# A reordered opening in a fused attention and MLP kernel: loads, memsets, one small copy and some transposes change their place

## The chip, the core and the metric

The kernel runs on one core of a Trainium2 chip. The core has TensorE (matmuls, PE in the profile), VectorE (DVE), ScalarE (ACT), GpSimd (POOL) and SyncE (SP), which only issues DMAs. Each engine works through its own instructions in the program's order; semaphores tie the engines together. The metric is the device time of the program in microseconds (us), over several executions.

## The reference

q, k and v are (8 batches, 8 heads, 576 positions, 64), f is (8, 8, 576); w_in is (512, 2048), w_out is (2048, 512), all float32.

```python
scores = q @ k.T / sqrt(64)                  # for each batch and head
cum = cumsum(log(clip(f, 0.0001, 1.0)))      # along the positions
scores = where(later position, -1e9, scores + cum[i] - cum[j])
attn = exp(scores - max); attn /= sum(attn) + 1e-9
x = (attn @ v), heads side by side           # (4608, 512)
h = x @ w_in
out = (h - tanh(h)) @ w_out                  # (4608, 512)
```

## The kernel before

**Pairs of heads.** The unit of attention is a pair of heads; a batch has four pairs (`NPAIR`), and `pairs` lists 32 of them in order. A pair's scores are computed transposed, positions of k on the partitions, in seven tiles (`TILES`): tiles 0 to 2 belong to the pair's first head, tile 3 holds the last 64 columns of both heads, tiles 4 to 6 belong to the second. `scores` (L337) makes one tile: matmuls of K^T and Q^T (L352), for batch 0 a matmul that adds the causal mask `late` (L355), and an exponential on ScalarE into a tile `e`, or `el` for tile 3 (L361). From batch 1 on GpSimd masks the tile instead (L371). `values` (L382) multiplies the tiles of the pair before with v (L389); VectorE divides by the sums (L398 to L400) into `xn`. `turn` (L407) transposes `xn` into `XR`, the input of the MLP: in batch 0 with TensorE (L417) and a copy on VectorE (L419) or ScalarE (L421), later by DMA.

**The decay in the matmul.** K^T and Q^T have 67 rows: 64 of the head and three more, which add the decay. For every head but the first of batch 0 the rows are filled by DMA from `chi` and `clo`, which are computed for all 64 heads at once: clip of f (L181), logarithm on ScalarE (L184), cumulative sum (L187), `chi` (L189), `clo` (L190). For head 0 three rows of `clo` are copied straight into `KT[0]` (L191), and ScalarE writes the rows of `QT[0]` (L572).

**How Q^T and K^T come about.** In the early part (pairs 0 to 4 and some more) `trans` (L287) transposes q or k of a pair with six TensorE transposes (L298) into one PSUM bank, and two copies (four, if split) bring it to `QT` or `KT`: the letters of its argument `copies` give each copy's engine, V for VectorE (L311), A for ScalarE (L309). With "VA" or "Vv" only the first copy is issued at once, and the others wait in `LATER` until `rest()` issues them.

**The order of work** is written out by hand. After some set-up, `start()` (L570) runs pair 0's transposes and its tiles 0 and 1, with filler matmuls (`unread`, whose results nobody reads). `bulk()` (L209) issues the remaining loads of batch 0. Then, for each pair p, `att_items(p)` (L591) lists what is emitted around each of its seven tiles `ti`: the scores, loads from the table `LOADS`, transposes of later pairs, values of the pair before, turns. For p up to 3 nothing else is there; from p = 4 steps of the MLP (`mlp1`, L441; `mlp2`, L506) are spread between them, and after the last pair the MLP's rest runs alone.

**Loads.** All loads of q, k, v and the weights are DMAs of GpSimd's queue: `load_qk` (L101), `load_v_rest` (L122), `load_v_head` (L126), `load_v_block` (L130), `load_win` (L221). GpSimd is busy for 0.6 to 1.2 us with the issue of each, and its other instructions wait behind it. The order for batch 0 is: q and k of heads 0-1 and 2-3, the last 64 positions of v, v's heads 0 and 1, the mask `late` (L169), the `chi` row of Q^T (L212), q and k of heads 4-5 and 6-7, four blocks of v. `last()` (L585), in pair 1, holds four memsets of GpSimd that batch 1 and `EL[2]` need.

Of the kernel before, what the change touches and what calls it, by code (L numbers as in the profile page):

```python
# [14 lines left out]
PITCH = 640  # L15
VW = 66
# [5 lines left out]
def kernel(  # L22
# [10 lines left out]
    nc = tc.nc  # L33
    P = 128
# [87 lines left out]
    def load_v_rest(b):  # L122
        nc.gpsimd.dma_start(out=vn[b % 2][0:S % P, NJ - 1, :, 0:D],
                            in_=v[b, :, S - S % P:S, :].rearrange("h p d -> p h d"))
# [40 lines left out]
    EL = [cst.tile([P, 192], FP16, tag=f"el{i}", name=f"el{i}") for i in range(3)]  # L165
    load_v_rest(0)
    load_v_head(0, 0)
    load_v_head(0, 1)
# [10 lines left out]
    for e in EL[0:2]:  # L179
        nc.vector.memset(e, 0.0)  # L180
    nc.vector.tensor_scalar(out=lf, in0=lf, scalar1=0.0001, scalar2=1.0,  # L181
                            op0=ALU.max, op1=ALU.min)
    nc.vector.memset(vn[0][:, :, :, D:VW], 1.0)
# [7 lines left out]
    nc.vector.tensor_copy(out=KT[0][NH:NX, 0, 0:S], in_=clo[NH:NX, :])  # L191
# [17 lines left out]
    def bulk():  # L209
        (k_hi, chi_0), (k_lo, clo_0), (q_hi, _) = aug_rows(0)  # L210
        nc.sync.dma_start(out=k_hi, in_=chi_0)
        nc.gpsimd.dma_start(out=q_hi, in_=chi_0)  # L212
        nc.sync.dma_start(out=k_lo, in_=clo_0)
        load_qk(qn, q, 0, 4, 6)
        load_qk(kn, k, 0, 4, 6)
        load_qk(qn, q, 0, 6, H)
        load_qk(kn, k, 0, 6, H)
        for n in range(NJ - 1):
            load_v_block(0, n, 2, H)
# [5 lines left out]
    def load_wout(e0, e1):  # L225
# [4 lines left out]
             (1, 0): [lambda: load_win(0, DFF // 2)],  # L230
# [56 lines left out]
    def trans(b, c, src, dst, early, copies, split=False):  # L287
# [26 lines left out]
        now = 1 if copies in ("VA", "Vv") else 2  # L314
# [255 lines left out]
    def start():  # L570
        unread(47)
        nc.scalar.activation(out=QT[0][NH:NX, 0, :], in_=cum[NH:NX, :], func=AF.Identity, bias=add_q[NH:NX, :], scale=mul_q[NH:NX, :])  # L572
        q_rest = trans(*pairs[0], qn, QT, True, "AAAA", True)
        for fn in q_rest:
            fn()
        unread(6)
        k_rest = trans(*pairs[0], kn, KT, True, "VVVV", True)
        unread(34)
        scores(*pairs[0], 0)
        for fn in k_rest:  # L580
            fn()
        scores(*pairs[0], 1)
        unread(2)

    def last():  # L585
        nc.gpsimd.memset(KT[1][:, :, S:PITCH], 0.0)
        nc.gpsimd.memset(vn[1][D:P, NJ - 1, :, :], 0.0)
        nc.gpsimd.memset(vn[1][:, :, :, D:VW], 1.0)
        nc.gpsimd.memset(EL[2], 0.0)

    def att_items(p):  # L591
        def put(fn, *args):
            items.append((lambda: fn(*args), True))
# [6 lines left out]
        for ti in range(len(TILES)):  # L600
# [12 lines left out]
            if ti == 5 and p < NPAIR - 1:  # L613
                put(trans, *pairs[p + 2], qn, QT, True, "VV")
# [11 lines left out]
            if ti == at_k and p < 2 * NPAIR - 1 and p != NPAIR:  # L626
                put(trans, *after, kn, KT, early, "AV" if p in (0, 2) else "VV")
            if p == NPAIR:
                if ti == 0:
                    put(turn, *pairs[1])  # L630
                elif ti == 1:
                    put(turn, *pairs[p - 2])
                    put(values, *before)
                    put(mlp1, 0, 0, 0)
                elif ti == 2:
                    put(mlp1, 0, 1, 0)
                    put(turn, *before, True)
                    put(trans, *after, kn, KT, early, "Vv")
            elif early and ti in (2, 4) and before:
                put(values, *before, (ti // 2 - 1,))  # L640
            elif not early and ti == 2 and before:
                put(values, *before, (0, 1), p == NPAIR + 2)
# [71 lines left out]
```

## Time and profile before

| | |
|---|---|
| time, 3 runs | 338.72 us median (338.71 to 339.28) |
| the profiled execution | 338.77 us, of which the span (first to last instruction) is 337.1 us |
| busy in the span | PE 330.0 (98%), DVE 260.8 (77%), ACT 233.2 (69%), POOL 163.2 (48%) |
| granted TensorE clock | 1.00 |
| first scores of pair 0 on TensorE | at 9.11 us |
| first scores of pair 4 on TensorE | at 24.78 us |
| first matmul with w_in | at 27.28 us |

Times inside the profile count from the start of the span. In a timeline a row has the start, the duration from first start to last end of a run of like instructions, the engine, the line of the kernel, the operation, what it writes and reads, its shape, the number of instructions, and in brackets the engine's idle time just before it and what ended that. In the view of waits a row names who waited for whom: microseconds in total, times, longest.

### The profile page before, as it was taken

What the parts mean: (1) busy time and instruction counts of PE and PEld (TensorE: products, weight loads), DVE (VectorE), ACT (ScalarE), POOL (GpSimd) and SP (SyncE); (2) the same over time, 40 slices, a digit from 0 to 9 for tenths busy, and PEclk for the clock granted to TensorE, in tenths of its full rate; (3) what the DMA queues carried; (4) which work ended last, traced back from release to release, by engine and by line L of the source; (5) the groups of instructions that cost most, each with busy time, mean ns of one, the idle gap of its engine ahead of it and who ended that gap; (6) DMA issues with size and microseconds to landing.
All of it is one profiled execution on the core that took longest, in us unless ns stands there. A gap on an engine that the chain in (4) does not pass through costs nothing.

```text
span 337.1 us, 8726 instructions
## 1 busy us (share of the span) xinstructions
PE 330.0 (98%) x3313; PEld 235.6 (70%) x3313; DVE 260.8 (77%) x509; ACT 233.2 (69%) x438; POOL 163.2 (48%) x321
## 2 busy tenths in 40 slices
PE   8899999999999999999999999999999999999996
PEld 8775558875687558845888888656865686486485
DVE  7998986659887886778867896788668866966865
ACT  6997777978977886788677867787558733632630
POOL 8977467775667564767377637722322210000000
PEclk9999999999999999999999999999999999999999
DMA  9999999999979997999899999990130022002003
GB/s 113 143 203 202 186 198 165 184 159 172 142 87 190 136 134 72 164 152 139 94 122 187 118 112 117 163 132 18 51 113 2 19 65 97 2 31 95 0 12 116
DMA packets 147468, 38.82 MB, mean 115 GB/s; under 512 B 128181, under 2 KB 146335, under 8 KB 147426
## 3 DMA queue, kind: packets, MB, share of 16 engines
q0 software_dynamic: 94528, 18.37, 75.5%
q1 hardware_dynamic: 52892, 19.89, 32.4%
q8 instruction: 26, 0.43, 0.6%
q14 instruction: 16, 0.13, 0.2%
q10 hardware_dynamic: 6, 0.01, 0.0%
HBM read 36.85 MB, written 9.44 MB: 137 GB/s over the span
## 4 chain that ended last, share of the span: by engine, by line
PE 90%; DVE 7%; ACT 2%; issue 1%; ACTq 0%
PE hps L451 36%; PE ops L517 29%; PE ps L352 11%; PE av L389 8%; PE ops L492 4%; DVE KT L311 2%; DVE QT L311 1%; PE t L298 1%; ACT e L361 1%; DVE xn L400 1%; DVE gq L462 0%; DVE TQ L187 0%; ACT th L456 0%; PE x L417 0%; DVE clo L190 0%
## 5 line engine op out<-in xcount | busy, mean ns | idle before, releaser
L451 PE MATMUL hps<-XR,win 128*128 128x512 f16 (+1 forms) x640 | 140.7, 357 | 0.3 <-DVE gq L462 0.3
L456 ACT ACTIVATE th<-hps 128x512 f32<-128x512 f32 x144 | 86.6, 602 | 55.5 <-PE hps L451 53.5
L361 ACT ACTIVATE e<-ps 128x512 f16<-128x512 f32 x192 | 110.2, 597 | 8.9 <-PE ps L352 7.4
L462 DVE TENSOR_TENSOR gq<-hps,th 128x512 f16<-128x512 f32 x144 | 98.0, 687 | 23.6 <-ACT th L456 22.0
L371 POOL TENSOR_SCALAR_AFFINE_SELECT e<-e 128x128 f16<-128x128 f16 x168 | 60.7, 364 | 71.5 <-ACT e L361 68.7
L451 PEld LDWEIGHTS <-win 128*128 128x128 f16 x640 | 57.7, 97 | 49.0 <-issue 1.1
L352 PE MATMUL ps<-QT,KT 67*128 67x64 f16 (+4 forms) x384 | 76.5, 276 | 2.0 <-DVE KT L311 1.4
L517 PEld LDWEIGHTS <-gq 128*128 128x128 f16 x640 | 60.3, 97 | 11.1
L517 PE MATMUL ops<-wout,gq 128*128 128x256 f16 x512 | 63.2, 272 | 0.0
L352 PEld LDWEIGHTS <-KT 67*128 67x128 f16 x384 | 36.4, 98 | 23.4 <-DVE KT L311 2.0
L389 PEld LDWEIGHTS <-e 128*128 128x128 f16 x896 | 32.3, 97 | 3.6
L389 PE MATMUL av<-vn,e 128*128 128x65 f16 x896 | 33.6, 193 | 0.0
L517 PE MATMUL ops<-W,sq 128*128 128x256 f16 x256 | 31.2, 272 | 0.0
L131 POOL DMA_DIRECT2D vn<-in_v_dram x32 | 28.0, 877 | 6.5 <-DMA win<-in_moe_w_in_dram 2.9
L400 DVE TENSOR_TENSOR xn<-av,rs 128x640 f16<-128x640 f32 x32 | 26.4, 825 | 1.3 <-DVE rs L399 0.2
L517 PEld LDWEIGHTS <-sq 128*128 128x128 f16 x256 | 24.1, 97 | 3.4
L108 POOL DMA_DIRECT2D kn<-in_k_dram x25 | 21.2, 848 | 2.1 <-issue 1.8
L108 POOL DMA_DIRECT2D qn<-in_q_dram x25 | 21.2, 848 | 1.8 <-issue 1.4
L371 POOL TENSOR_SCALAR_AFFINE_SELECT el<-el 128x128 f16<-128x128 f16 x28 | 9.3, 333 | 26.1 <-ACT el L361 25.8
L398 DVE TENSOR_SCALAR rs<-av 128x10 f32<-128x10 f32 x32 | 5.2, 163 | 18.2 <-PE av L389 17.0
L532 ACT ACTIVATE m<-ops 128x512 f32<-128x512 f32 x16 | 9.5, 596 | 10.9 <-PE ops L517 10.9
L484 DVE TENSOR_TENSOR gq<-gq 128x512 f16<-128x512 f16 x32 | 17.1, 533 | 0.0
(83 smaller groups left out, 311.8 us busy)
## 6 DMA issues: line engine op xcount, KB each, us to landing
out_dram<-ost SPq DMA_DIRECT2D x34, 256.0 KB
vn<-in_v_dram POOLq DMA_DIRECT2D x24, 128.0 KB, 6.2
qn<-in_q_dram POOLq DMA_DIRECT2D x20, 128.0 KB, 5.0
kn<-in_k_dram POOLq DMA_DIRECT2D x20, 128.0 KB, 5.6
win<-in_moe_w_in_dram POOLq DMA_DIRECT2D x2, 1024.0 KB, 11.8
wout<-in_moe_w_out_dram POOLq DMA_DIRECT2D x2, 1024.0 KB, 15.6
XR<-xn SPq DMA_TRANSPOSE x56
qn<-in_q_dram POOLq DMA_DIRECT2D x6, 144.0 KB, 4.6
```

The costliest lines, as they stand in the source:

```text
L108: nc.gpsimd.dma_start(out=dst[b % 2][0:pn, n, :].rearrange("p (h d) -> p h d", h=H), in_=src[b, :, n * P:n * P + pn, :].rearrange("h p d - ...
L131: nc.gpsimd.dma_start(out=vn[b % 2][:, n, h0:h1, 0:D], in_=v[b, h0:h1, n * P:(n + 1) * P, :].rearrange("h p d -> p h d"))
L352: nc.tensor.matmul(out=ps[:, col:col + n], lhsT=kt[0:rows, h, j * P:(j + 1) * P], rhs=qt[0:rows, h, i0:i0 + n], start=True, stop=cut == 0)
L361: nc.scalar.activation(out=e[:, lo:hi], in_=ps[:, lo:hi], func=AF.Exp, bias=-SHIFT, scale=qscale)
L371: nc.gpsimd.affine_select(out=view, in_=view, compare_op=ALU.is_ge, fill=0.0, base=0, pattern=pat, channel_multiplier=-1)
L389: nc.tensor.matmul(out=av[:, a, ib, :], lhsT=E.pop((b, c, a, j, ib)), rhs=vn[b % 2][:, j, 2 * c + a, 0:D + 1], start=(j == 0), stop=(j == ib))
L400: nc.vector.tensor_tensor(out=xn.rearrange("p i (a d) -> p a i d", a=2), in0=av[:, :, :, 0:D], in1=rs.to_broadcast([P, 2, NJ, D]), op=ALU. ...
L451: nc.tensor.matmul(out=hps[:, o:o + n], lhsT=win[:, ci, ft * P:(ft + 1) * P], rhs=XR[:, ci, t:t + n], start=(ci == 0), stop=(ci == NCH - 1))
L456: nc.scalar.activation(out=th, in_=hps, func=AF.Tanh, scale=-1.0)
L462: nc.vector.tensor_tensor(out=GQ[(u, i)][:, half, kt, :], in0=hps, in1=th, op=ALU.add)
L484: nc.vector.tensor_tensor(out=LHS[name](u, i)[:, ks], in0=LHS[x](u, i)[:, ks], in1=LHS[y](u, i)[:, ks], op=op)
L517: nc.tensor.matmul(out=ps[:, m, :], lhsT=LHS[lhs](u, kt // 4)[:, kt % 4, m * P:(m + 1) * P], rhs=rhs[:, kt, :], start=(fresh and (apart or ...
```

## The change

- In the set-up, q's heads 4 and 5 are loaded first, then v's head 0, then the last positions of v. v's head 1 moves into `bulk()`, behind k's heads 4 and 5.
- All three `EL` memsets stand behind the clip of f; `last()` no longer has the third.
- The DMA of the `chi` row moves from `bulk()` to just behind `clo`, and GpSimd, not VectorE, copies the three rows of `clo` into `KT[0]`.
- The memsets of `KT[1]` and `vn[1]` move from GpSimd to VectorE; that of `KT[1]` to `start()`, between pair 0's tiles 0 and 1.
- w_in's first half is loaded in two pieces of a quarter.
- The filler ahead of the first scores has 29 matmuls in place of 34.
- Transposes: pair 2's q moves from pair 0's tile 5 to its tile 3, with its second copy issued later; pair 1's second K^T copy is issued between those two. Pair 3's and pair 4's q move from tile 5 to tile 6 of the pairs 1 and 2.
- In pair 2, the values of pair 1's first head follow tile 3, not tile 2.

```diff
-    load_v_rest(0)
+    load_qk(qn, q, 0, 4, 6)
     load_v_head(0, 0)
-    load_v_head(0, 1)
+    load_v_rest(0)
...
-    for e in EL[0:2]:
-        nc.vector.memset(e, 0.0)
     nc.vector.tensor_scalar(out=lf, in0=lf, scalar1=0.0001, scalar2=1.0,
                             op0=ALU.max, op1=ALU.min)
+    for e in EL:
+        nc.vector.memset(e, 0.0)
...
-    nc.vector.tensor_copy(out=KT[0][NH:NX, 0, 0:S], in_=clo[NH:NX, :])
+    nc.gpsimd.dma_start(out=QT[0][D + 2:D + 3, 1:H, :], in_=chi[1:H, :])
+    nc.gpsimd.tensor_copy(out=KT[0][NH:NX, 0, 0:S], in_=clo[NH:NX, :])
...
     def bulk():
-        (k_hi, chi_0), (k_lo, clo_0), (q_hi, _) = aug_rows(0)
+        (k_hi, chi_0), (k_lo, clo_0), _ = aug_rows(0)
         nc.sync.dma_start(out=k_hi, in_=chi_0)
-        nc.gpsimd.dma_start(out=q_hi, in_=chi_0)
         nc.sync.dma_start(out=k_lo, in_=clo_0)
-        load_qk(qn, q, 0, 4, 6)
         load_qk(kn, k, 0, 4, 6)
+        load_v_head(0, 1)
...
-             (1, 0): [lambda: load_win(0, DFF // 2)],
+             (1, 0): [lambda: load_win(0, DFF // 4), lambda: load_win(DFF // 4, DFF // 2)],
...
-        now = 1 if copies in ("VA", "Vv") else 2
+        now = 1 if copies in ("VA", "Vv", "Av") else 2
...
-        unread(34)
+        unread(29)
         scores(*pairs[0], 0)
         for fn in k_rest:
             fn()
+        nc.vector.memset(KT[1][:, :, S:PITCH], 0.0)
         scores(*pairs[0], 1)
...
     def last():
-        nc.gpsimd.memset(KT[1][:, :, S:PITCH], 0.0)
-        nc.gpsimd.memset(vn[1][D:P, NJ - 1, :, :], 0.0)
-        nc.gpsimd.memset(vn[1][:, :, :, D:VW], 1.0)
-        nc.gpsimd.memset(EL[2], 0.0)
+        nc.vector.memset(vn[1][D:P, NJ - 1, :, :], 0.0)
+        nc.vector.memset(vn[1][:, :, :, D:VW], 1.0)
...
-            if ti == 5 and p < NPAIR - 1:
+            if ti == 6 and 0 < p < NPAIR - 1:
                 put(trans, *pairs[p + 2], qn, QT, True, "VV")
...
-                put(trans, *after, kn, KT, early, "AV" if p in (0, 2) else "VV")
+                put(trans, *after, kn, KT, early, "Av" if p == 0 else "AV" if p == 2 else "VV")
+            if p == 0 and ti == 3:
+                put(trans, *pairs[2], qn, QT, True, "Vv")
+                items.append((rest, False))
...
-            elif early and ti in (2, 4) and before:
-                put(values, *before, (ti // 2 - 1,))
+            elif early and ti in (3 if p == 2 else 2, 4) and before:
+                put(values, *before, (ti // 4,))
```

More of the change, by code (lines that the diff above doesn't have):

```diff
@@ L165 @@
     EL = [cst.tile([P, 192], FP16, tag=f"el{i}", name=f"el{i}") for i in range(3)]
+    load_qk(qn, q, 0, 4, 6)
+    load_v_head(0, 0)
     load_v_rest(0)
-    load_v_head(0, 0)
-    load_v_head(0, 1)
     nc.gpsimd.affine_select(out=late, in_=late, compare_op=ALU.is_ge, fill=-60000.0,
```

## The prediction

> **What bounds the kernel now.** I read the page's slices first, then TensorE's waits by stretch, then the timelines of VectorE (DVE), ScalarE (ACT) and GpSimd (POOL) over the first 35 us. The slices (one digit is 8.4 us, busy tenths):
>
> ```profile
> PE   8899999999999999999999999999999999999996
> DVE  7998986659887886778867896788668866966865
> ```
>
> TensorE is full except in the first two slices and the last. From 60 us on its row in the table of windows reads 10.00 of 10.00 us up to the tail, so what the change can win or lose lies before about 50 us, and whatever it wins there stays won, since all later work follows TensorE. TensorE's waits in the windows 0:10, 10:20 and 20:30:
>
> ```profile
> PE idle L566 <- DVE warm L142: 1.1, 1, 1.1
> PE ps L352 <- DVE KT L311: 0.9, 1, 0.9
> ...
> PE ps L352 <- ACT e L361: 0.3, 1, 0.3
> PE idle L566 <- ACT el L361: 0.2, 1, 0.2
> ...
> PE ps L352 <- DVE KT L311: 0.4, 1, 0.4
> PE x L417 <- DVE xn L400: 0.2, 1, 0.2
> ```
>
> The reader should see that 0.9 (the first scores) and 0.4 both end on a copy of K^T by VectorE. In VectorE's timeline (start, duration, instruction, idle before it):
>
> ```profile
> 3.60 0.25 DVE L180 MEMSET el<- 128x96 uint32 x2
> 3.77 0.39 DVE L181 TENSOR_SCALAR TQ<-TQ 67x576 f32<-67x576 f32 x1
> 4.91 1.35 DVE L187 TENSOR_TENSOR_SCAN TQ<-TK,TQ 67x576 f32<-67x576 f16 x1 [0.66 <-ACT TQ L184]
> ...
> 7.76 0.30 DVE L191 COPY KT<-clo 3x576 f16<-3x576 f16 x1
> 8.09 1.97 DVE L311 COPY KT<-t 64x288 f16<-64x288 f16 x4
> 10.26 1.62 DVE L311 COPY QT<-t 64x576 f16<-64x576 f16 x2 [0.20 <-PE t L298]
> 12.22 0.81 DVE L311 COPY KT<-t 64x576 f16<-64x576 f16 x1 [0.34 <-ACT KT L309]
> ...
> 23.10 1.62 DVE L311 COPY KT<-t 64x576 f16<-64x576 f16 x2
> ```
>
> Between 8.09 and 24.72 VectorE idles only twice, 0.20 and 0.34 us. The last row is pair 4's K^T, and TensorE's first scores of pair 4 start at 24.78, 0.43 us late, on it. **So VectorE's queue is the bound from the first K^T copy to 24.78**; TensorE's smaller waits before that are slack. A gain at the start counts only as far as this queue ends earlier.
>
> **The change, part by part.** All times are of the profiled execution: 338.77 us, of which the span is 337.1 and 1.7 lie around it; it is 0.05 above the median of 338.72.
>
> *Start of the chain.* The two memsets of `EL` stand ahead of the clip of the decays (3.60 and 3.77 in the rows above; the clip's input was there, its wait had ended by 3.5). Moved behind, the clip starts at 3.60: 0.17 earlier. The three memsets then lie in the 0.66 idle ahead of the scan (3 x 0.14 = 0.42, with the ones of `vn` 0.12: 0.54), so the added third one costs nothing; without that cover it would cost 0.14. The scan, chi and clo follow 0.17 earlier: clo ends at 7.56 instead of 7.73.
>
> *Decay rows to GpSimd.* The copy of L191 leaves VectorE: 7.76 to 8.09 is 0.33. The K^T copies then start at 8.09 - 0.17 - 0.33 = 7.59. The scores need the first two (0.97 in all, 8.56) and the copied rows. No GpSimd copy is in this trace. Its nearest rows:
>
> ```profile
> 6.48 0.55 POOL L169 TENSOR_SCALAR_AFFINE_SELECT late<-late 128x128 f16<-128x128 f16 x1
> 7.17 0.54 POOL L212 DMA_DIRECT2D QT<-chi x1
> ...
> 17.49 0.60 POOL L586 MEMSET KT<- 67x512 f16 x1
> 18.15 0.53 POOL L587 MEMSET vn<- 64x528 f16 x1
> 18.74 0.18 POOL L588 MEMSET vn<- 128x80 f16 x1
> ```
>
> Memsets of 80 and 512 elements give 0.98 ns an element and 0.10 fixed, so 0.66 for 576. The selects of L371 (128 elements 0.30, 256 elements 0.42) give 0.73. From above, the select of `late` took 0.55 for 128 elements, beside chi on VectorE: at that rate 576 cost 2.46. I take 0.73: a select also reads and writes SBUF. Before it in GpSimd's queue stand three loads (0.68 + 0.79 + 0.71, for 0.71 + 0.77 + 0.77 now), the select and the chi row's DMA, which is done at about 7.5. The copy runs from 7.60 to 8.33, covered by the K^T copies until 8.56. First scores: 8.56 + 0.05 = 8.61 for 9.11. Five filler matmuls fewer (0.06 each) end at 7.9, inside that wait, and cost nothing.
>
> *Memsets of batch 1 to VectorE.* `KT[1]`'s stands behind pair 0's K^T copies: 0.37 from start to next start (the row of L159). Pair 1's Q^T copies could start at 8.61 + 1.14 = 9.75 (now 9.11 to 10.25); VectorE is free at 7.59 + 1.96 + 0.37 = 9.92. So the idle of 0.20 goes, and these copies start 0.33 earlier. The two of `vn[1]` (rows of L163 and L183) cost 0.31 + 0.12 = 0.43, in pair 1, with nothing to hide them. The four memsets leave GpSimd's queue (1.56).
>
> *Late turns.* Pair 2's Q^T is transposed in pair 0's tile 3, and its first copy goes ahead of pair 1's second K^T copy, which waited 0.34 for ScalarE's. That idle goes: 11.55 Q^T of pair 2, 12.37 K^T of pair 1, 13.2 the other half. Late next: pair 1's first scores, which need the K^T copy ended at 13.2. Now it ends at 13.03 and they start at 13.50, held by other waits; they can't follow the 0.5 of the start. That is a new wait of some 0.3 on TensorE, within the slack. Pair 2's K transposes behind it end near 13.25 + 0.70 = 13.95, VectorE wants them at 14.02. The turns moved from tile 5 to 6 and pair 1's values moved to tile 3 change TensorE's order inside the slack (17.2 to 24.4): nothing.
>
> *Loads.* q's heads 4 and 5, issued at 4.3 with landings there taking 4.4 to 4.8, are in by 9.1, wanted at 11. Behind the GpSimd copy are kn 4-5, v head 1, q and k 6-7, four v blocks. v head 1 moves from 5.73 to 9.0; its 4.6 to landing makes 13.6, wanted at 15.2. The last v block is issued 0.8 later (13.5), and lands between 17.6 (the DMA engines, not the issue, set it: their latency grew from 3.4 to 5.2 us here) and 18.45; wanted at about 18.5. A miss falls into TensorE's 0.30 and 0.43. w_in's half takes one issue more (0.83), paid by the memsets that left; it landed at 26.1, its first matmul is at 27.28, and the first quarter alone can land earlier. Nothing.
>
> *Sum at 24.72:* -0.33 (pair 1's copies) - 0.34 (idle) + 0.43 (memsets) = **-0.24**. TensorE's scores of pair 4 then start at 24.54, and later work keeps the distance: 338.77 - 0.24 = **338.5**. The 0.50 at the start is half spent again on VectorE's memsets.
>
> **The rivals.**
>
> *The gain is eaten (338.8).* Tile 3 of pair 0 needs the chi row of Q^T over GpSimd's queue, issued at 7.17 and 3.7 us to landing: 10.87, against a first use at 11.13. The change wants it at 10.6, and puts 144 KB in place of 64 KB ahead of it; at the windows' 166 GB/s that is up to 0.5 later. Then tile 3 stays near 11.1, pair 2's Q transposes behind it end at 11.8 instead of 11.55, and VectorE loses the 0.25. For it: the margin is 0.26 now and about none after. Against: the issue itself comes 0.2 earlier.
>
> *More than the queue allows (337.8).* If VectorE's memsets overlap its copies and TensorE's waits after 24.78 (0.16 on xn, 0.32 on gq at 33.38) go too: 0.50 + 0.48. Against: both end on VectorE's queue, and its rows show no overlap beyond 0.04.
>
> *Slower: the GpSimd copy itself (339.9).* TensorE's first scores wait for it, everything behind. Pair 1's copies start at its end + 0.05 + 1.14 once that is past 9.92, and 10.16 is where the sum is zero: a copy of over 1.4 us loses. At the rate of the `late` select, 2.46, it ends at 10.06, pair 1's copies start at 11.25, and the sum is 1.00 - 0.34 + 0.43 = +1.1. For it: that select ran beside chi and took 0.55 where the one of `id` took 0.29. Against: GpSimd's memsets at 17.5 to 19.0 ran beside VectorE's copies out of PSUM, as this copy would, and both kept their usual durations. A first use of an instruction could also cost extra; the nearest row is ScalarE's table load, 1.28, which would make the copy 2.0 and the time 339.4. The Trainium skill, GPSIMD Engine Reference, Instruction dispatch, says that the first call of a freshly loaded kernel pays some 6 us that no profile row shows; by that, as an estimate, the copy ends at 14.3 and the time is 344. The trace does not bear it out: GpSimd's first select, 0.29 us, started at 1.22, right after its input.
>
> **Chances.** Forecast 0.55 (its own range 338.4 to 338.65); eaten 0.24; more 0.09; slower by the copy 0.12, a third of that within the bound. About 0.2%, 0.68 us, is what a measurement of this kernel can tell from no change. So faster 0.09, same 0.83, slower 0.08. The range of 338.0 to 339.0 takes in the first two and half a copy's excess, and leaves out the long copy and most of the large gain.
>
> **What would show it.** L181 at 3.6; the K^T copies at 7.6; a GpSimd COPY of about 0.7 that ends before 8.6; the first scores at 8.6; no idle of VectorE until 24.5; a new wait of TensorE for K^T near 13.2; pair 4's scores at 24.5. Wrong if the copy takes over 1.4, if tile 3's scores stay at 11.1, or if TensorE waits for a v block near 18.

## The result and the profile after

| | before | after |
|---|---|---|
| time, median of 6 (lowest to highest) | 338.76 us (338.71 to 339.28) | 340.12 us (339.75 to 340.28) |
| profiled execution, its span | 338.77, 337.1 | 340.10, 338.3 |
| first scores of pair 0, first matmul | 9.12 | 9.08 |
| first scores of pair 4, first matmul | 24.78 | 25.02 |
| TensorE's idle time at L517, near 105 us | none | 0.97 |

The ratio is 1.0035 [1.0022, 1.0048] (in brackets the 95% interval): the changed kernel is slower by 1.36 us. The forecast was 338.5, and the range ended at 339.0. Between the two profiled executions the span grew by 1.2 us. Two places hold it: 25.02 - 24.78 = 0.24 in the opening, and 0.97 at 105 us, in a part of the kernel that the change does not touch and where the prediction expected nothing to move. (The 9.11 in the table of the kernel before is the start of the weight load of that first matmul.)

The busy slices of the page, TensorE and VectorE, of the kernel after:

```profile
PE   8899999999998999999999999999999999999996
DVE  7998986659788887688967786688667766966865
```

The new 8 in TensorE's thirteenth slice (101 to 110 us) is the 0.97. The waits of TensorE in the windows 0:10, 20:30 and 100:110 give the sizes:

```profile
PE ps L352 <- DVE KT L311: 0.8, 1, 0.8
...
PE ps L352 <- DVE KT L311: 0.7, 1, 0.7
PE x L417 <- DVE xn L400: 0.2, 1, 0.2
...
PE ops L517 <- DVE ost L536: 1.0, 1, 1.0
```

The wait for pair 4's K^T has grown from 0.4 to 0.7; the last row is new. First the opening, in VectorE's timeline after:

```profile
3.82 0.68 DVE L179 TENSOR_SCALAR TQ<-TQ 67x576 f32<-67x576 f32 x1 [0.18 <-DMA TQ<-in_f_dram]
4.46 0.35 DVE L182 MEMSET el<- 128x96 uint32 x3
5.25 1.35 DVE L187 TENSOR_TENSOR_SCAN TQ<-TK,TQ 67x576 f32<-67x576 f16 x1 [0.34 <-ACT TQ L184]
...
7.98 1.96 DVE L311 COPY KT<-t 64x288 f16<-64x288 f16 x4
9.92 0.27 DVE L582 MEMSET KT<- 67x256 uint32 x1
10.21 2.52 DVE L311 COPY QT<-t 64x576 f16<-64x576 f16 x3
...
23.34 1.61 DVE L311 COPY KT<-t 64x576 f16<-64x576 f16 x2
```

The clip (first row) did not start at 3.60. It had to wait for the load of f, which landed at 3.71 (3.44 in the kernel before, by the trace's semaphores), and it took 0.68 where it had taken 0.39. So the scan began at 5.25, not at 4.74, and the K^T copies at 7.98, not at 7.59. From there on the queue is as the prediction has it: one memset behind the K^T copies, then three copies without a gap. From the first scores to pair 4's it is 25.02 - 9.08 = 15.94; the forecast was 24.54 - 8.61 = 15.93, and in the kernel before it was 24.78 - 9.12 = 15.66. **So the opening gave up its gain at the clip and then paid about what was forecast for the rest.** That the two agree to 0.01 is partly luck: from the first K^T copy to pair 1's Q^T copies it took 0.10 less than forecast, and the rest as much more.

For the 0.97 GpSimd's timeline is the place to begin. After:

```profile
6.26 0.42 POOL L169 TENSOR_SCALAR_AFFINE_SELECT late<-late 128x128 f16<-128x128 f16 x1
7.51 0.54 POOL L191 DMA_DIRECT2D QT<-chi  x1 [0.82 <-DVE chi L189]
8.21 0.66 POOL L192 COPY KT<-clo 3x576 f16<-3x576 f16 x1 [0.17 <-DVE clo L190]
8.82 0.67 POOL L102 DMA_DIRECT2D kn<-in_k_dram  x1
...
14.80 0.69 POOL L102 DMA_DIRECT2D qn<-in_q_dram  x1
...
17.31 1.61 POOL L222 DMA_DIRECT2D win<-in_moe_w_in_dram  x2
```

The same two loads before:

```profile
13.53 0.68 POOL L102 DMA_DIRECT2D qn<-in_q_dram  x1
...
16.05 0.83 POOL L222 DMA_DIRECT2D win<-in_moe_w_in_dram  x1
```

GpSimd now stands still for 0.82 and 0.17 while VectorE makes chi and clo, and copies for 0.66. Batch 1's first load is issued 14.80 - 13.53 = 1.27 later, and w_in 1.26: the chi row's DMA comes 0.34 later (7.51 for 7.17), the wait for clo and the copy add 0.77 (8.05 to 8.82), and the issues behind them 0.16. What this does to the transfers shows in the page's row of GB/s, before and then after (40 slices of 8.4 us):

```profile
GB/s 113 143 203 202 186 198 165 184 159 172 142 87 190 136 134 72 164 152 139 94 122 187 118 112 117 163 132 18 51 113 2 19 65 97 2 31 95 0 12 116
```

```profile
GB/s 113 119 189 201 187 196 173 179 151 150 143 131 145 160 154 81 157 153 133 107 124 172 129 114 109 166 135 15 50 115 4 19 66 96 2 31 94 2 10 116
```

In the second and third slice 24 + 14 = 38 GB/s are missing, over 8.4 us some 0.32 MB. From the fourth slice on the two rows run alike, at 165 to 202 for the next 40 us: nothing is made good there, and 0.32 MB at 200 GB/s is 1.6 us. The page's busy share of the DMA engines is 8 or 9 tenths in all these slices, so the row shows that they moved less, not that they stood idle. The lag can be followed through the trace:

| | before | after |
|---|---|---|
| batch 1's k of heads 4 to 7 landed | 29.15 | 31.38 |
| w_out's second load landed | 55.18 | 59.70 |
| third q block of batch 3 issued | 56.38 | 60.00 |
| last k block of batch 3 landed | 72.00 | 78.89 |
| first transposing load of TK issued on SP's queue | 79.11 | 80.15 |
| last transposing load of TK issued on SP's queue | 84.36 | 86.66 |
| VectorE's copy of K^T from TK (L120) began | 91.83 | 94.16 |
| VectorE's add into `ost` (L536) began | 103.54 | 105.35 |

The lag grows at 60 us, where GpSimd's queue itself stands still until w_out's second load has landed. GpSimd's timeline after:

```profile
60.00 0.89 POOL L108 DMA_DIRECT2D qn<-in_q_dram  x1 [3.28 <-DMA wout<-in_moe_w_out_dram]
```

In the kernel before this load is issued without such a wait. In all eighteen traces a DMA of GpSimd's queue is issued only when the eighth before it has landed: never more than eight are under way, and each standing still of this kind ends with the landing of the eighth before. So a late landing makes later issues late. VectorE's timeline after, at the last two rows of the table:

```profile
94.16 0.51 DVE L120 COPY KT<-TK 64x1152 f16<-64x1152 f16 x1 [2.02 <-DMA TK<-kn]
...
105.35 0.68 DVE L536 TENSOR_TENSOR ost<-ops,u 128x512 f32<-128x512 f32 x1
```

VectorE waits 2.02 for the last transposing load of TK; its whole queue is late; and at 105 TensorE needs the buffer that the add frees. The transposing load did not wait for k in this trace: the last k block had landed at 78.89, before the first of the five was issued at 80.15. They were late on SP's queue. The first was held 1.04, by work ahead of it, and two of the five took longer to issue than the 1.22 of the kernel before (chain that ended last, after):

```profile
82.81 1.70 SPq L113
...
84.60 1.97 SPq L113
...
86.66 7.47 DMA TK<-kn
```

At that time loads of v were still landing, up to 87.87 (82.78 before), since they are issued behind the k blocks. That these slowed the transposing loads fits, and was not tried by itself.

### The profile page after: what moved, and what is told of

It reads as the page before. It is cut to its first block, busy times and chain, and to the rows that moved or that the text cites. A ratio compares the mean times of both kernels' runs of the same rounds, so it can differ in the third digit from the quotient of the medians.

```text
span 338.3 us, 8717 instructions
## 1 busy us (share of the span) xinstructions
PE 330.2 (98%) x3308; PEld 235.8 (70%) x3308; DVE 262.0 (77%) x512; ACT 232.9 (69%) x438; POOL 164.8 (49%) x319
## 4 chain that ended last, share of the span: by engine, by line
PE 81%; DVE 8%; ACT 3%; DMA 3%; SPq 2%; issue 1%; DVEq 0%; ACTq 0%
PE hps L451 32%; PE ops L517 26%; PE ps L352 10%; PE av L389 7%; PE ops L492 4%; DMA TK<-kn 2%; SPq L113 2%; DVE KT L311 2%; PE t L298 1%; ACT e L361 1%; DVE QT L311 1%; DVE sq L484 1%; DVE xn L400 1%; DMA TQ<-in_f_dram 1%; DVE gq L462 1%
## 5 line engine op out<-in xcount | busy, mean ns | idle before, releaser
L371 POOL TENSOR_SCALAR_AFFINE_SELECT e<-e 128x128 f16<-128x128 f16 x168 | 61.5, 371 | 66.8 <-ACT e L361 64.6
L517 PEld LDWEIGHTS <-gq 128*128 128x128 f16 x640 | 60.4, 97 | 12.1 <-issue 1.1
L517 PE MATMUL ops<-wout,gq 128*128 128x256 f16 x512 | 63.2, 272 | 1.0 <-DVE ost L536 1.0
L517 PE MATMUL ops<-W,sq 128*128 128x256 f16 x256 | 31.2, 272 | 0.0
L517 PEld LDWEIGHTS <-sq 128*128 128x128 f16 x256 | 24.1, 98 | 3.4
L398 DVE TENSOR_SCALAR rs<-av 128x10 f32<-128x10 f32 x32 | 5.2, 162 | 17.5 <-PE av L389 16.4
```

The costliest lines, as they stand in the source:

```text
L371: nc.gpsimd.affine_select(out=view, in_=view, compare_op=ALU.is_ge, fill=0.0, base=0, pattern=pat, channel_multiplier=-1)
L517: nc.tensor.matmul(out=ps[:, m, :], lhsT=LHS[lhs](u, kt // 4)[:, kt % 4, m * P:(m + 1) * P], rhs=rhs[:, kt, :], start=(fresh and (apart or ...
```

## The experiments

Four theories stand in the expectations. **L**: GpSimd issues batch 1's loads late while few transfers are under way, the DMA engines run short, and since their queue is full afterwards the lag is carried to 105 us. **S**: the additional load of w_in's first half does it. **V**: VectorE's queue alone, longer by its new memsets, is what is late at 105. **D**: any delay of GpSimd costs, wherever it stands. Each experiment's kernel was timed ten times, except where another number stands, beside the kernel before on the same chip (medians 338.80 to 338.88). "After" and "before" ahead of a diff name the kernel that was edited. Where a memset of `W1` is added, it is useless work on a weight tile that is loaded later; no experiment leaves out a part of the computation.

**One part at a time.** w_in's first half in one load again, in the kernel after:

```diff
-             (1, 0): [lambda: load_win(0, DFF // 4), lambda: load_win(DFF // 4, DFF // 2)],
+             (1, 0): [lambda: load_win(0, DFF // 2)],
```

> The changed kernel with w_in's first half in one load again. Theory L (late issue): in the opening GpSimd waits for chi and clo and then copies, so that every load behind is issued 1.3 us later, the DMA engines run short between 8 and 20 us, and the lag is still there at 94 us, where VectorE waits 2.0 us for K^T's transposed block. By L the second piece of w_in costs only its own issue of 0.8: 339.9 to 340.2, the wait of TensorE near 105 us stays. Theory S (split): the extra load and its smaller packets, or the changed turn in which loads wait for earlier loads, make the lag: 339.0 to 339.2, the wait near 105 us is gone.

339.17 us (338.76 to 339.69), ratio 1.0007 [0.9997, 1.0016]. That is the time of theory S, and L's forecast for this run was missed. The wait at 105 fell to 0.23, VectorE's for TK to 1.56. The opposite edit, the split alone in the kernel before:

> The kernel before with w_in's first half in two loads and nothing else. Theory L: 338.7 to 338.9, no wait near 105 us. Theory S: 339.6 to 339.9, a wait of TensorE of 0.8 to 1.0 near 105 us.

338.86 (338.76 to 339.56), 1.0002 [0.9993, 1.0011], and no wait at 105. **S alone is false**: the split costs nothing in the kernel before. But in the kernel after, whose loads are already late, it costs about 1.0 (1.36 above the kernel before with it, 0.29 without), so it has its part there. One load more also moves, for each later load, which one is the eighth before it; in the kernel before with the split the last k block of batch 3 landed at 76.86 for 72.00, without a cost. Next the `clo` rows by VectorE, in the kernel after:

```diff
-    nc.gpsimd.tensor_copy(out=KT[0][NH:NX, 0, 0:S], in_=clo[NH:NX, :])
+    nc.vector.tensor_copy(out=KT[0][NH:NX, 0, 0:S], in_=clo[NH:NX, :])
```

> The changed kernel with the three rows of clo copied by VectorE again; the chi row's DMA keeps its new place. GpSimd is free 0.8 us earlier (0.17 of waiting, 0.66 of copy). Theory L: the loads behind are issued 0.8 earlier and a good part of the 0.97 near 105 us goes, while VectorE's queue ends 0.3 later at pair 4: 339.4 to 339.8. Theory S: the wait near 105 us stays and VectorE's 0.3 come on top: 340.3 to 340.5.

339.40 (338.87 to 339.85), 1.0013 [1.0004, 1.0023]. Batch 1's first load is issued at 13.75, and the wait at 105 is gone, although VectorE has 0.3 more to do and pair 4's scores start 0.09 later than in the kernel after (25.11). **This speaks against V.** And the copy alone, in the kernel before:

```diff
-    nc.vector.tensor_copy(out=KT[0][NH:NX, 0, 0:S], in_=clo[NH:NX, :])
+    nc.gpsimd.dma_start(out=QT[0][D + 2:D + 3, 1:H, :], in_=chi[1:H, :])
+    nc.gpsimd.tensor_copy(out=KT[0][NH:NX, 0, 0:S], in_=clo[NH:NX, :])
...
-        nc.gpsimd.dma_start(out=q_hi, in_=chi_0)
```

> The kernel before with the three rows copied by GpSimd, behind the chi row's DMA, and nothing else. VectorE's first K^T copy comes 0.3 earlier, which should bring pair 4's scores 0.2 to 0.3 forward. Theory L: loads are 0.8 later, a wait for late K^T blocks appears near 92 to 106 us: 338.8 to 339.5. Theory S: no such wait, 338.4 to 338.6.

338.86 (338.50 to 339.95), 1.0002 [0.9993, 1.0011]. The median is that of the kernel before, but the executions are spread over 1.45 us, and the profiled one was the slowest of them. It issued the first load at 14.32 and shows TensorE's waits that L would have (windows 20:30 and 100:110):

```profile
PE hps L451 <- DMA win<-in_moe_w_in_dram: 0.4, 1, 0.4
...
PE ops L517 <- DVE ost L536: 0.7, 1, 0.7
```

GpSimd stood still for w_out there too, for 3.36 at 60 us, and VectorE waited 2.05 for TK: in this execution the copy alone makes the same chain as in the kernel after. This kernel seems to stand at an edge, over it in some executions and not in others; only this one of the ten was traced.

**Delays and mended versions.** A memset of 1.2 us on GpSimd ahead of q's heads 4 and 5, in the kernel before:

```diff
     def bulk():
...
         nc.sync.dma_start(out=k_lo, in_=clo_0)
+        nc.gpsimd.memset(W1[:, 0:5, :], 0.0)
         load_qk(qn, q, 0, 4, 6)
```

> The kernel before with one useless GpSimd instruction, a memset of 128 x 1280 elements into a weight tile that is written much later (by the other memsets some 1.35 us), between the chi row's DMA and the load of q's heads 4 and 5. No VectorE, TensorE or ScalarE instruction changes. Theory L: every load behind is issued 1.35 later, the last block of k for batch 3 lands some 5 us later than in the kernel before (72.0), VectorE waits for its transpose near 92 us and TensorE for VectorE near 105 us by 0.5 to 1.1: 339.3 to 339.9. Theory V (what costs is VectorE's own longer queue in the opening): 338.7 to 338.9, no wait near 105 us.

339.85 (339.73 to 343.83), 1.0051 [1.002, 1.0082], in L's range for another reason. This answers nothing about late loads, for there was no wait at 105. The memset fell on VectorE's copy of the decay rows (GpSimd's timeline, then VectorE's):

```profile
7.69 1.19 POOL L214 MEMSET W<- 128x1280 f16 x1
```

```profile
7.76 1.29 DVE L191 COPY KT<-clo 3x576 f16<-3x576 f16 x1
```

The copy takes 0.30 in the kernel before; here 1.29, and the first scores begin at 10.10. Next, k's heads 4 and 5 loaded while GpSimd would wait for chi, in the kernel after:

```diff
+    load_qk(kn, k, 0, 4, 6)
     nc.gpsimd.dma_start(out=QT[0][D + 2:D + 3, 1:H, :], in_=chi[1:H, :])
...
-        load_qk(kn, k, 0, 4, 6)
         load_v_head(0, 1)
```

> The changed kernel with the load of k's heads 4 and 5 moved ahead of the chi row's DMA, into the 0.6 to 0.8 us in which GpSimd waits for chi. The loads behind are issued 0.65 earlier, and VectorE's opening stays. Theory L: the wait near 105 us falls from 0.97 to 0.2 to 0.5: 339.2 to 339.7. Theory V: 340.1, unchanged.

339.66 (339.03 to 340.19), 1.0018 [1.0008, 1.0028]. No wait at 105, but another at 11.2, for pair 0's tile 3 (TensorE's waits, window 0:20):

```profile
PE ps L352 <- DMA QT<-chi: 1.4, 1, 1.4
```

The view names the chi row of Q^T, which, behind one more load of 144 KB, landed at 11.98 (10.33 in the kernel after). But by the trace's semaphores the two decay rows of K^T on SP's queue landed later still, at 12.16 and 12.35 (10.27 and 10.44 in the kernel after), and the scores began at 12.59. So tile 3 waited for its decay rows, as in the rival "the gain is eaten", and for those of K^T last. TensorE's delay of 1.4 also hides what may be left at 105, so this run says little about L. Next, batch 1's memsets on GpSimd, in pair 3, behind its first load of v:

```diff
-        nc.vector.memset(KT[1][:, :, S:PITCH], 0.0)
...
-        nc.vector.memset(vn[1][D:P, NJ - 1, :, :], 0.0)
-        nc.vector.memset(vn[1][:, :, :, D:VW], 1.0)
+        nc.gpsimd.memset(KT[1][:, :, S:PITCH], 0.0)
+        nc.gpsimd.memset(vn[1][D:P, NJ - 1, :, :], 0.0)
+        nc.gpsimd.memset(vn[1][:, :, :, D:VW], 1.0)
...
-            if p == 1 and ti == 3:
-                put(last)
...
+            if p == 3 and ti == 0:
+                items.append((last, False))
```

> The changed kernel with the three memsets of batch 1 on GpSimd, but in the stretch in which it waits for a load of w_in to land (behind the first v block of batch 1). VectorE's queue loses some 0.8 us in the opening: pair 4's scores at 24.1 to 24.3 in place of 25.0. Theory L: the late k blocks land at the same absolute time, so TensorE only waits longer near 105 us (1.6 to 1.8 in place of 0.97): 339.9 to 340.2, nothing gained. Theory V: 339.3 to 339.5.

343.23 (342.89 to 343.77, four executions), 1.0126 [1.0111, 1.0142], far above both forecasts. That place was not idle. GpSimd was held by the landing of an earlier load, the memset of `KT[1]` ran at 26.04, and pair 4's K^T copies had to wait for it (VectorE's timeline):

```profile
26.60 1.60 DVE L311 COPY KT<-t 64x576 f16<-64x576 f16 x2 [3.75 <-POOL KT L586]
```

One number of it is of use. Here f landed early, at 3.47: the clip began at 3.57, the K^T copies at 7.51 and the first scores at 8.62, near the forecast for the change (3.60, 7.59, 8.61). All repairs together, on the kernel after: this edit, the one of k's heads 4 and 5, and with them

```diff
+    for e in EL[0:2]:
+        nc.vector.memset(e, 0.0)
     nc.vector.tensor_scalar(out=lf, in0=lf, scalar1=0.0001, scalar2=1.0,
                             op0=ALU.max, op1=ALU.min)
-    for e in EL:
-        nc.vector.memset(e, 0.0)
+    nc.vector.memset(EL[2], 0.0)
...
-             (1, 0): [lambda: load_win(0, DFF // 4), lambda: load_win(DFF // 4, DFF // 2)],
+             (1, 0): [lambda: load_win(0, DFF // 2)],
```

> The changed kernel with all of it mended: k's heads 4 and 5 ahead of the chi row, batch 1's memsets on GpSimd in its idle stretch, w_in's first half in one load, two EL memsets ahead of the clip again. Theory L: pair 4's scores near 24.0 (0.7 to 0.8 before those of the kernel before), loads 0.5 later than in the kernel before, the wait near 105 us 0 to 0.8 with the run: 338.0 to 338.7. Theory V: 338.0 in every run, no wait near 105 us.

339.57 (339.24 to 340.01), 1.002 [1.001, 1.0029], above both forecasts. TensorE waited 0.72 for tile 3 from 11.2, until VectorE's copy of Q^T and the `clo` row of K^T were there, both at 11.68; VectorE waited 0.24 for the memset of `KT[1]`; pair 4's scores began at 25.51, and there was nothing at 105.

**L against D and V.** The useless memset of 1.2 us again, in the kernel before, where no copy on VectorE is beside it. Once ahead of batch 1's first load, once behind its q of heads 4 to 7:

```diff
-    LOADS = {(0, 1): [lambda: load_qk(qn, q, 1, 0, 2), lambda: load_qk(kn, k, 1, 0, 2)],
+    LOADS = {(0, 1): [lambda: nc.gpsimd.memset(W1[:, 0:5, :], 0.0), lambda: load_qk(qn, q, 1, 0, 2), lambda: load_qk(kn, k, 1, 0, 2)],
```

> The kernel before with a useless GpSimd memset of 1.2 us (128 x 1280 elements) ahead of batch 1's first q load, at 13.5 us; VectorE then copies only out of PSUM, so that its instructions should keep their durations. Loads wait there some 4.5 us from issue to landing. Theory L: the DMA engines run short for about 1.2 us, batch 1's loads and all later ones land later, and the last block of k for batch 3 is late near 92 us: TensorE waits 0.2 to 1.0 near 105 us, 339.0 to 339.8. Theory V (only VectorE's queue in the opening counts): 338.7 to 338.9. Theory D (a delay of GpSimd counts wherever it stands): like L here.

```diff
-             (1, 2): [lambda: load_qk(qn, q, 1, 4, H)],
+             (1, 2): [lambda: load_qk(qn, q, 1, 4, H), lambda: nc.gpsimd.memset(W1[:, 0:5, :], 0.0)],
```

> The same memset behind the load of q's heads 4 to 7 of batch 1, at 17.5 us, where 10 us of loads are already queued. Theory L: the DMA engines have work for 10 us, so nothing is late and the time is that of the kernel before, 338.7 to 338.9. Theory V: the same. Theory D: 339.0 to 339.8, as in the run with the memset at 13.5.

GpSimd's timelines, of the early memset and then of the later one:

```profile
13.53 1.21 POOL L228 MEMSET W<- 128x1280 f16 x1
14.64 0.68 POOL L102 DMA_DIRECT2D qn<-in_q_dram  x1
...
17.16 0.84 POOL L222 DMA_DIRECT2D win<-in_moe_w_in_dram  x1
```

```profile
16.05 0.83 POOL L222 DMA_DIRECT2D win<-in_moe_w_in_dram  x1
...
17.49 1.24 POOL L231 MEMSET W<- 128x1280 f16 x1
```

The early one: 339.35 (338.98 to 340.30), 1.0017 [1.0008, 1.0027]. The later one: 338.78 (338.75 to 339.18), 0.9999 [0.9989, 1.0008]. **The same 1.2 us of GpSimd cost 0.53 ahead of 14 us and nothing at 17.5: D is false, and late loads cost time while VectorE's queue in the opening is the same in both, which L asks for and V excludes.** The traces show why the later one is free: GpSimd would have stood still anyway, until w_in landed, and the memset takes its time from that. Its next load stood still for 2.92 in the kernel before (issued at 26.43), and here:

```profile
26.66 0.83 POOL L131 DMA_DIRECT2D vn<-in_v_dram  x1 [2.05 <-DMA win<-in_moe_w_in_dram]
```

The early memset stands ahead of w_in's own issue, and moves its landing. That one's first scores are at 9.12, as before, and w_in landed at 28.01 in place of 26.14. TensorE's waits, window 20:30:

```profile
PE hps L451 <- DMA win<-in_moe_w_in_dram: 0.6, 1, 0.6
```

So the lag need not wait for 105 us, where L had forecast it: here the whole first half of w_in, still one load, is the first to be wanted. In the kernel after its first quarter landed alone, at 24.64, and no wait for w_in came. Then the change with the order of `EL` and w_in whole as in all repairs together, and its memsets back on GpSimd in their old place; once with the first two lines of this diff (the copy on VectorE) and once without them:

```diff
-    nc.gpsimd.tensor_copy(out=KT[0][NH:NX, 0, 0:S], in_=clo[NH:NX, :])
+    nc.vector.tensor_copy(out=KT[0][NH:NX, 0, 0:S], in_=clo[NH:NX, :])
...
-        nc.vector.memset(KT[1][:, :, S:PITCH], 0.0)
...
-        nc.vector.memset(vn[1][D:P, NJ - 1, :, :], 0.0)
-        nc.vector.memset(vn[1][:, :, :, D:VW], 1.0)
+        nc.gpsimd.memset(KT[1][:, :, S:PITCH], 0.0)
+        nc.gpsimd.memset(vn[1][D:P, NJ - 1, :, :], 0.0)
+        nc.gpsimd.memset(vn[1][:, :, :, D:VW], 1.0)
```

> The changed kernel with VectorE copying clo's rows, batch 1's memsets in GpSimd's old place at 17.5 us, w_in's first half in one load, and two EL memsets ahead of the clip again; new load order and late turns stay. VectorE loses the two idle stretches and pays nothing for memsets. Theory L: loads behind at most 0.2 later than in the kernel before, no wait near 105 us; pair 4's scores at 24.3 to 24.5: 338.2 to 338.5. Theory D: the same opening, and a wait of some 0.4 near 105 us.

> As the run before, but with the copy of clo's rows on GpSimd. VectorE's queue is 0.33 shorter still: pair 4's scores at 24.0 to 24.2. Theory L: loads 0.9 to 1.0 later than in the kernel before, TensorE waits 0.2 to 1.2 near 105 us, more in some runs than in others: 338.3 to 339.3, so the copy on GpSimd loses what it wins. Theory V: 338.0 to 338.2 in every run.

Copy on VectorE: 339.09 (338.92 to 343.01), 1.002 [0.9997, 1.0043]: no wait at 105, but above the forecast. Pair 4's scores start at 25.10, not near 24.4. VectorE has less to do and idles instead:

```profile
10.41 1.62 DVE L312 COPY QT<-t 64x576 f16<-64x576 f16 x2 [0.20 <-PE t L299]
12.24 0.80 DVE L312 COPY QT<-t 64x576 f16<-64x576 f16 x1 [0.21 <-PE t L299]
...
16.60 0.17 DVE L399 TENSOR_SCALAR rs<-av 128x10 f32<-128x10 f32 x1 [0.31 <-PE av L390]
```

It waits for TensorE's transposes and values, so it was not the only bound of this stretch. Copy on GpSimd: 339.25 (338.55 to 340.37), 1.0013 [1.0003, 1.0024]; pair 4's scores at 24.56, but the first load is issued at 14.65, w_in lands at 28.08, and TensorE waits 0.90 for it. In this execution the loads take back what the copy gives in the opening.

**Earlier issues, VectorE's work unchanged.** Batch 1's first four loads merged into two, so that what follows is issued earlier, in the kernel after, with the kernel before as control. The number of loads under way changes with it:

```diff
-    LOADS = {(0, 1): [lambda: load_qk(qn, q, 1, 0, 2), lambda: load_qk(kn, k, 1, 0, 2)],
-             (0, 4): [lambda: load_qk(qn, q, 1, 2, 4), lambda: load_qk(kn, k, 1, 2, 4)],
+    LOADS = {(0, 1): [lambda: load_qk(qn, q, 1, 0, 4)],
+             (0, 4): [lambda: load_qk(kn, k, 1, 0, 4)],
```

> The changed kernel with batch 1's first four loads (q and k of heads 0-1, 2-3) merged into two (q of heads 0-3, k of heads 0-3). Same bytes, two issues of GpSimd fewer, so w_in and all behind are issued some 1.2 us earlier. Theory L: the wait near 105 us is gone or under 0.3, the opening stays: 339.0 to 339.3. If the lag came from somewhere else than the time of issue: 339.9 to 340.2.

> The kernel before with the merged loads alone. Its loads were never late, so earlier ones bring nothing: 338.6 to 338.9 by theory L.

339.20 (338.93 to 339.84), 1.0011 [1.0002, 1.0021], and the control 338.81 (338.76 to 338.89), 0.9998 [0.9989, 1.0008]. In the kernel after, the edit leaves 0.40 of the 1.36, and no wait at 105, with VectorE's work untouched. **V is false for the wait at 105**, as the copy alone, which makes VectorE's queue shorter, has shown too. The edit has a price of its own, since the merged k is wanted at 21.56 and lands at 22.74:

```profile
PE t L298 <- DMA kn<-in_k_dram: 1.2, 1, 1.2
```

Such a delay of TensorE would hide a wait of 0.97 by itself. But VectorE's copy of K^T from TK begins at 92.92 without a wait, 1.24 earlier than in the kernel after, so TK did come earlier.

Then the `EL` memsets alone in their old order, in the kernel after:

```diff
+    for e in EL[0:2]:
+        nc.vector.memset(e, 0.0)
     nc.vector.tensor_scalar(out=lf, in0=lf, scalar1=0.0001, scalar2=1.0,
                             op0=ALU.max, op1=ALU.min)
-    for e in EL:
-        nc.vector.memset(e, 0.0)
+    nc.vector.memset(EL[2], 0.0)
```

> The changed kernel with two EL memsets ahead of the clip again (the third behind it). If the clip's place is what cost the first scores: the clip starts at 3.77 and takes 0.39 to 0.42 in every run, first scores at 8.8 to 8.9 in place of 9.08, pair 4's at 24.7 to 24.8. Theory L: that gain is not seen in the end, because TensorE waits the longer near 105 us: 339.7 to 340.1. Without theory L: 339.8 at most and a wait unchanged.

And the merged loads in the mended kernel with the copy on GpSimd:

```diff
-    LOADS = {(0, 1): [lambda: load_qk(qn, q, 1, 0, 2), lambda: load_qk(kn, k, 1, 0, 2)],
-             (0, 4): [lambda: load_qk(qn, q, 1, 2, 4), lambda: load_qk(kn, k, 1, 2, 4)],
+    LOADS = {(0, 1): [lambda: load_qk(qn, q, 1, 0, 4)],
+             (0, 4): [lambda: load_qk(kn, k, 1, 0, 4)],
```

> The kernel of the last mended run (copy on GpSimd, memsets in GpSimd's old place, w_in's half in one load, EL memsets ahead of the clip) with batch 1's first four loads merged into two. Theory L: the delay of the copy is paid back by the two issues saved; no wait for w_in near 27 us, none near 105: pair 4's scores at 24.55 as in that run, 338.4 to 338.7. Otherwise 339.0 to 339.5, as without the merge.

With the old order: 339.19 (338.73 to 341.32), 1.0024 [1.0006, 1.0042], below L's forecast, with first scores at 9.07 and pair 4's at 24.94, both later than forecast. Six executions lie at 338.73 to 339.24 and four at 340.36 to 341.32; the profiled one, 338.91, has no wait at 105. That looks like the edge again, within one kernel; none of the four was traced. With everything: 339.27 (338.84 to 339.83), 1.0013 [1.0004, 1.0023], and 1.33 of waiting for the merged k, so L's 338.4 to 338.7 was missed.

The issues and landings of the profiled executions side by side:

| kernel | batch 1's first load issued | its k 4-7 landed | TensorE's waits for it |
|---|---|---|---|
| before, split alone | 13.52 | 30.56 | none |
| before, later memset | 13.53 | 29.74 | none |
| before | 13.53 | 29.15 | none |
| after, copy on VectorE | 13.75 | 29.12 | none |
| mended, copy on VectorE | 13.85 | 29.38 | none |
| before, copy on GpSimd | 14.32 | 31.22 | 0.4 w_in, 0.3 k, 0.72 at 105 |
| after, w_in whole | 14.60 | 30.14 | 0.23 at 105 |
| after, old order of `EL` | 14.63 | 30.20 | none |
| before, early memset | 14.64 | 31.10 | 0.60 w_in |
| mended, copy on GpSimd | 14.65 | 31.04 | 0.90 w_in |
| after | 14.80 | 31.38 | 0.97 at 105 |

In these rows no such wait came up to 13.85; from 14.3 on some have one and some do not. The runs left out had TensorE delayed by 0.7 or more in the opening, or are the control with merged loads. VectorE waits for TK in four of the eighteen traces: after (2.02), before with the copy on GpSimd (2.05), after with w_in whole (1.56), before with the early memset (0.79). They are the four in which at least one of TK's five transposing loads took over 1.5 us to issue; in the fourteen others the longest took 1.22 to 1.30. No version beat the kernel before by what can be measured.

## Why the prediction was wrong

Inside the span the forecast was -0.24 and the result is +1.2. Of the difference of 1.44, the loads are 0.97, and 0.47 is that the first scores came at 9.08 and not at 8.61.

**"Loads. ... Nothing."** This is the step that failed, by 0.97. The prediction asked of each moved load whether it would land before its own first use, and that was right: no wait for q, k or v of batch 0 came. It did not ask when the loads *behind* them in the queue would now be issued. It had the numbers for it: "the last v block is issued 0.8 later (13.5)" stands in its text (it was 1.27, at 13.99, for the chi row's DMA came later as well), and batch 1's first load is the next in that queue. But it followed only the block, and held the one more issue for w_in against the four memsets that left (1.56), and those stood at 17.5, where the delay experiments show that 1.2 us of GpSimd are worth nothing. The costs lie before 14 us, where the same 1.2 us cost 0.53 by themselves. What the runs showed in place of "nothing": loads issued 1.27 later, GpSimd standing still for 3.28 at 60 us behind a late one of w_out, TK's transposing loads late by 2.30, and TensorE waiting 0.97 at 105. That the late issue is the cause is shown by the runs that take it away (copy on VectorE) or make it alone (early memset; copy on GpSimd, in the execution that was traced); the second piece of w_in has its part in it, and the link from the late loads to SP's transposing loads is argued. The step "later work keeps the distance" fell with it: the slices showed a TensorE that was full after 60 us, not how near its suppliers were to being late.

**"Start of the chain", 0.17 earlier: a chance, counted as a certainty.** "The clip's input was there" held for one trace. In the eighteen traces f landed at 3.43 to 3.71, in the kernel after the latest of all. With the new order the clip began at 3.57 to 3.82, as f landed, and with the old order always at 3.77 or 3.78: the two memsets ahead of it had covered that spread. It took 0.68 in the profiled execution of after and 0.45 or 0.46 in the five others of the new order, for 0.39. Nor does an early f give the gain by itself. In the run with the memsets in pair 3 the first scores came at 8.62, against the forecast 8.61. In the one with the copy back on VectorE the clip began at 3.59 too, but the K^T copies only at 8.15, for 8.09 in the kernel before: chi took longer (0.58 in the kernel before), beside the select of `late`, which stands 0.2 earlier in the changed queue (VectorE's timeline):

```profile
6.18 0.75 DVE L189 TENSOR_SCALAR chi<-TQ,per 67x576 f16<-67x576 f32 x1
```

**"Decay rows to GpSimd": size right.** The copy took 0.66 for 0.73, beside VectorE's copies out of PSUM. The rival "slower: the GpSimd copy itself" did not happen: it ended at 8.87, and the scores waited for K^T. The Trainium skill's 6 us (GPSIMD Engine Reference, Instruction dispatch) for a first call of a freshly loaded kernel did not show: the copy started 0.16 after clo was done, took 0.66, and is the first of its kind in the kernel. What this part does cost is GpSimd's wait for chi and clo with all loads behind it, a wait that the prediction priced for the scores alone.

**"Memsets of batch 1 to VectorE": near.** From the first K^T copy to pair 1's Q^T copies it was 10.21 - 7.98 = 2.23, forecast 9.92 - 7.59 = 2.33; the stretch as a whole came out at 15.94 for 15.93.

**"Late turns ... That idle goes": not shown, and the sum came out with luck.** The idle times of 0.20 and 0.34 did go in the kernel after, the one filled by the memset of `KT[1]`, the other by pair 2's Q^T copy. But in the mended run with the copy on VectorE, which has the late turns and not the memsets, idle times of 0.20, 0.21 and 0.31 came instead, on TensorE's transposes and values, and from the first scores to pair 4's it was 25.10 - 9.28 = 15.82, for 15.66 in the kernel before. There the late turns won nothing. So the memsets, counted as a cost, seem to have filled idle time that the late turns, counted as a gain, had not taken away. That VectorE's queue alone is the bound from the first K^T copy to 24.78 was too strong. ScalarE, whose exponentials the values need, has no idle time over 0.2 from 9.8 to 27.4, in that run as in the kernel before; that it is the other bound is argued from its rows and was not tried.

**"The gain is eaten".** It was not at work in the kernel after, where the chi row landed at 10.33. With one more load ahead of that row TensorE did wait 1.4 for tile 3, but for the decay rows of SP's queue last, which the rival did not name.

What stays open: why the same kernel falls on either side of the edge from one execution to the next (the landings of f alone spread by a quarter of a microsecond); why the costs do not add up, since taking back any one of the split, the copy, the order of `EL` or the number of loads leaves 0.3 to 0.5 of the 1.36 over the kernel before of the same chip, and so returns 0.8 to 1.1; what slows the issue of TK's transposing loads; and where the 0.3 to 0.5 lie. In the kernel before with the split alone k 4-7 landed at 30.56 and the last k block of batch 3 at 76.86 without a wait at 105, so these landings by themselves do not decide.

## What to carry to other kernels

Price an instruction on the engine that issues DMAs by what stands behind it in that queue, up to the place where the queue next stands still for a landing. Here 1.2 us ahead of the load whose landing ended that wait cost 0.53, and the same 1.2 us behind it cost nothing. So take the sum of such a queue place by place, and follow a delay through the later loads, not only to the first use of the load that was moved. The rule is not complete: one more load at 18 us was free in the kernel before and cost about 1.0 in the kernel after. And an input that "is there in time" in one trace may be so only because something small stands ahead of it: look at the spread of the landing before the cover is removed.

## What the runs showed of the hardware

**VectorE and GpSimd slow each other between SBUF operands.** The copy of 3x576 took 0.30 alone and 1.29 beside a GpSimd memset of 1.19, and it ended 0.17 after the memset. VectorE's copies out of PSUM beside GpSimd's memsets kept their usual 0.80 each. The Trainium skill, SBUF — State Buffer, "SBUF: two separate sides", says that the two engines share a pair of ports, and that of a GpSimd instruction and a VectorE instruction in one of certain modes the one that starts first holds it for its whole length; the delayed copy agrees. Another pair agrees in part. Where the select of `late` started 0.18 behind chi, chi took 0.575 and the select 0.54, so the select ended 0.15 after chi, less than the 0.29 of a select of that size elsewhere: they overlapped. Where it started less than 0.1 behind, chi took 0.71 to 0.75 and the select 0.33 or 0.34, as if the select had gone first.

**The clip had three durations.** Always with GpSimd issuing loads beside it, the same 67x576 elements took 0.39 to 0.42 when it started at 3.77 or 3.78, behind the `EL` memsets, 0.45 or 0.46 in five profiled executions of the new order, and 0.68 in the one of the kernel after. A collision with one of those issues is possible, and was not tried by itself.

**An idle engine can be the late one.** GpSimd did nothing for 0.82 us but wait for chi, and the chi row's DMA, with every load behind it, came 0.34 later than in the kernel before. At 60 us it stood still for 3.28, with at most eight of its loads under way. The profile shows both as idle time of an engine that is busy for 49% of the span.

**A first use cost nothing:** GpSimd's first copy of the kernel took 0.66 for 576 elements on three partitions; the line through its memsets of 80 and 512 elements gives 0.66 for the same number.
